# Moving waits in a fused attention and Fourier-mixing kernel: masks, last fold, square root, requests and closing work

## The chip, the core and the metric

The kernel runs on one core of a Trainium2 chip. The core has five engines that run their own instruction queues in order: TensorE (PE, matrix products into PSUM), VectorE (DVE), ScalarE (ACT), GpSimd (POOL) and SyncE (SP), which here only issues transfers. They meet through semaphores. The metric is the device time of one execution in microseconds (us); lower is better.

## The reference

```python
scores = scale * np.matmul(q, k.transpose(0, 1, 3, 2))   # q, k, v: (8, 8, 576, 64)
thresh = np.max(scores, axis=-1, keepdims=True) - tau
scores = np.where(scores >= thresh, scores, -1e9)
attn = softmax(scores)                                    # denominator + 1e-9
x = np.matmul(attn, v)                                    # heads laid side by side: (8, 576, 512)
u = x + np.real(np.fft.fft(np.fft.fft(x, axis=1), axis=2))
un = (u - mean(u)) / np.sqrt(var(u) + 1e-6)               # over the last axis
out = u + np.maximum(un @ w_ch1, 0.0) @ w_ch2             # w_ch1: 512 x 2048, w_ch2: 2048 x 512
```

Everything is float32.

## The kernel before

The eight batches go through two pipelines that are interleaved by hand on each engine's queue.

**Attention.** A batch has four pairs of heads, a pair five steps (t = 0 to 4): four tiles of 128 query rows for both heads, and one for the last 64 rows of both. Step i has its scores in PSUM (L427, L433; tile `sc`), then in `softmax_first` the row maxima on VectorE (L506) and the exponentials and the threshold on ScalarE (L512, L516), in `softmax_second` the masks, which also sum the rows, on VectorE (L527) with the reciprocal (L534), and in `softmax_third` the scaling on ScalarE (L540). `weights_in_parts` transposes the weights of the step before on TensorE (L578, L596; tiles `pe`, `pw`) and copies them out on ScalarE (L584, L598). `values_in_parts` multiplies them with v at t = 3 and at t = 1 of the next pair (L627, tile `pv`) and copies the result to x on ScalarE (L634). `prep_pair` (t = 3) transposes k and q of the next pair on VectorE (L398 to L401) and then calls `load_pair` for the pair behind it, which has 8 transfers on SyncE's queue (L134); `load_v` has four (L149, L152).

**Mixing.** When a pair is complete, `fold_rows` adds and subtracts its rows in mirrored places (L678, L683); for the last pair of a batch this is on VectorE and `mixing` follows at once: more folds (L709 to L740), products with the Fourier tables (L750, tile `py`; L767, L771, tile `pa`), sums and differences (L787, L788) and the addition to x that gives u (`add`, L790, L794), on GpSimd.

**Channels.** Of the 4608 rows of u, groups of 512 go through the two products. The first group is done plainly; its weights are then kept in memory in the form for a fast multiplication scheme (seven products for eight, for the second product in two levels). Groups 1 to 8 run `two_level`: sums of u on GpSimd (`u_form`, L1085), seven products for each of four parts (L1161, tile `ph`, evictions at L1098, L1170, L1103), and 49 products of the second level (L1278, tile `po`), whose left sides are formed at L1142 and L1119 on VectorE and GpSimd and whose results are gathered in `v_..` (evictions L1290, L1292, L1295; sums L1209, L1268) and added to u with the factor 1/sqrt(var) (`rows.add`, L861). `Rows.load` transposes u into rows (L834, L839, L840, statistics L842); `Rows.factors` has the square root on ScalarE, [...] loads of tables stand before and behind it (L850, L853), and the reciprocal (L854). Weight blocks of 1 MB are read again for every group into three buffers (`ensure`, L1034), each requested when the buffer's last product has been issued.

The loop for steps 40 and later sets the order: scores, values, softmax_first, then `fill`, which takes the next piece of `mixing` and as many pieces of `two_level` as a budget of work allows, masks, half of the transposes, `fill`, the other half, scaling, `fill`. Folds advance at `fold_more`, which is also called as background work inside `two_level`. All single-bank products share four PSUM banks (tag `mm`); the scores have two buffers of two banks. Behind the loop `fill` alone runs the rest; the sums and additions of the last group are all done behind its last product:

```python
        for v in (v_22, v_21, v_12):
            pending.extend(gather(V if last else P, v))
        ...
        if g == NG - 1:
            while pending:
                tick()
```

Of the kernel before, what the change touches and what calls it, by code (L numbers as in the profile page):

```python
# [47 lines left out]
def kernel(  # L48
# [12 lines left out]
    nc = tc.nc  # L61
# [329 lines left out]
    def prep_pair(n):  # L391

        q_raw, k_raw = loaded.pop(n)
        kT = sb.tile([128, D + S], FP32, tag="kT", name="kT")
        nc.vector.transpose(kT[:, D : D + S], k_raw[:, :])  # L398
        nc.vector.transpose(kT[64:128, 0:D], k_raw[64:128, 512:S])
        qT = sb.tile([128, S], FP32, tag="qT", bufs=1, name="qT")  # L400
        nc.vector.transpose(qT[:, :], q_raw[:, :])  # L401
        heads[n] = (qT, kT, v_in[n % 2])
        if n + 1 < B * NPAIR:
            load_pair(n + 1)

    def prep_ends(n):
# [312 lines left out]
    def mixing(b):  # L719
# [58 lines left out]
        for t in range(2):  # L778
            cols = slice(128 * t, 128 * t + 128)
            tmp = sb.tile([128, 3, KH], FP32, tag="tmp", bufs=1, name="tmp")  # L780
            low, high, sin = (tmp[:, c, :] for c in range(3))
            pb = over_seq(y_o, 1, cols, 128)
            nc.scalar.copy(sin, pb[:, 0:KH])
            yield MIX / 11
            pa = over_seq(y_e, 0, cols, 128)

            nc.vector.tensor_tensor(out=low, in0=pa[:, 0:KH], in1=sin, op=ALU.subtract)  # L787
            nc.vector.tensor_tensor(out=high, in0=pa[:, 0:KH], in1=sin, op=ALU.add)  # L788
            def add(c, rows, first, second, eng=nc.gpsimd):
# [270 lines left out]
    def two_level(g, rows):  # L1060
# [21 lines left out]

        def u_form(out_, in0, in1):
            for c in range(2):
                nc.gpsimd.tensor_tensor(  # L1085
                    out=out_[:, c], in0=in0[:, c], in1=in1[:, c], op=ALU.subtract
                )

# [119 lines left out]
        def plus(eng, to, other):  # L1208
            return lambda: eng.tensor_tensor(out=to, in0=to, in1=other, op=ALU.add)  # L1209
# [15 lines left out]
            ]  # L1225

        def finish(i, n, v):
            v = v.rearrange("p (j n) -> p j n", n=128)
            cols = slice(256 * n, 256 * n + 256)
            second = v[:, 3]  # L1230
            second = bass.AP(
                tensor=second.tensor, offset=second.offset,
                ap=[list(second.ap[0]), [-128, 2], [1, 128]],
            )
            return [
                lambda: rows.add(2 * i, cols, v[:, 1:7:5]),
                lambda: rows.add(2 * i + 1, cols, second),
            ]
# [27 lines left out]
        at_slots(4, (0, 2), finish(0, 0, v_11))  # L1266
        at_slots(
            5, (0,), [lambda: P.tensor_tensor(out=v_12, in0=v_u, in1=v_22, op=ALU.add)]  # L1268
        )
        at_slots(6, (0, 1), [plus(P, v_22, v_u), plus(P, v_21, v_u)])  # L1270
        for at, m in enumerate(L1):
            for jn, j in enumerate(J):
                if jn in (0, 4):
                    bank = ps.tile([128, 512], FP32, tag="mm", bufs=4, name="po")
                to = bank[:, 128 * (jn % 4) : 128 * (jn % 4 + 1)]
                right_ = block(g, True, 7 * at + jn)
                for s in range(4):
                    nc.tensor.matmul(  # L1278
                        to, lefts[m][j][:, s], right_[:, 128 * s : 128 * (s + 1)],
                        start=jn in (0, 4) and s == 0, stop=s == 3, skip_group_check=True,  # L1280
                    )
                if jn in (3, 6):
                    size = 512 if jn == 3 else NV - 512
                    src = bank[:, 0:size]

                    def here(v):
                        return v[:, 0:512] if jn == 3 else v[:, 512:NV]

                    if m in (1, 5, 4):
                        nc.scalar.copy(here({1: v_u, 5: v_22, 4: v_21}[m]), src)  # L1290
                    elif m == 2:
                        V.tensor_tensor(out=here(v_11), in0=here(v_u), in1=src, op=ALU.add)  # L1292
                    else:
                        to = here(v_12 if m == 3 else v_u)
                        V.tensor_tensor(out=to, in0=to, in1=src, op=ALU.add)  # L1295
# [12 lines left out]
        last = g == NG - 1  # L1308
        for v in (v_22, v_21, v_12):
            pending.extend(gather(V if last else P, v))  # L1310
# [5 lines left out]
        if g == NG - 1:  # L1316
            while pending:
                tick()
        yield 2048

    pending = []

    def tick():

        for _ in range(2):
            if pending:
                pending.pop(0)()
# [14 lines left out]
            fold_more()  # L1342

    late = []


    mixes = []
# [17 lines left out]
    total = B * per_batch  # L1365
    groups = 0
# [220 lines left out]
    for i in range(2 * per_batch, total + 3):  # L1587


        n, t = divmod(i, NT)  # L1590
        values = iter(())
        if i < total:
            scores(i)
        if t == 3 and i < total:
            values = values_in_parts(n, 0)
        elif t == 1 and n > 0:
            while folds:
                fold_more()
# [18 lines left out]
        if t > 2 or i % per_batch == 1:  # L1617
            fold_more()
        fill()
        if i % per_batch == 1:  # L1620
            fold_more()
        next(weights, None)
        if i < total:
            softmax_third(i)
            if t == 1:
                prep_ends(n)
            if t == 2 and n + 1 < B * NPAIR:
                scale_q(n + 1)
            if t == 3 and n + 1 < B * NPAIR:
                prep_pair(n + 1)  # L1630
        if i % per_batch == 1:
            fold_more()
        fill()
    per_slot = cost(0) / 40
    while mixes or work:
        fill()
# [46 lines left out]
```

## Time and profile before

| what | value |
|---|---|
| time, median of 3 runs | 1615.85 us (1615.81 to 1615.89) |
| span of the profiled execution | 1612.0 us |
| TensorE busy | 1541.6 us |
| VectorE, ScalarE, GpSimd busy | 1086.8, 906.5, 826.6 us |
| TensorE's mean granted clock | 0.987 of full |
| read from memory, written | 207.5 MB, 29.6 MB |
| last matmul ends | 1600.7 us |

A line of a timeline gives the start, the length of a run of like instructions, the engine, the line of the code, output and inputs, how many there were and, in brackets, how long the engine had been idle and what released it. A line of the waits gives who waited for whom: us in total, times, longest. A line of the windows view gives a stretch, the busy time in it, the clock that TensorE was granted (1.00 is full), the share of the transfer engines in use and GB/s. A busy TensorE is not one at its peak: at half clock its matmuls take longer and count as busy.

### The profile page before, as it was taken

To read this page: it belongs to the slowest core of one execution; us is meant where nothing else is said; L and a number is where in the kernel's file an instruction comes from. 1 tells how busy PE (TensorE), PEld (TensorE's weight loads), DVE (VectorE), ACT (ScalarE), POOL (GpSimd) and SP (SyncE) were. 2 spreads that over 40 slices of the span, in tenths; PEclk is the share of its full clock that TensorE was granted. 3 is DMA by queue.
4 is the path that set the end of the run, shared out by engine and by line. 5 is a ranking of instruction groups with operands and counts; after the bars stand their busy time and mean duration, and the time that the engine had idled before them with its cause. 6 is when DMAs were issued, how large, how long until landed. Compare 5 with 4: busy or idle time off the path is not lost.

```text
span 1612.0 us, 27099 instructions
## 1 busy us (share of the span) xinstructions
PE 1541.6 (96%) x9770; PEld 1191.6 (74%) x9770; DVE 1086.8 (67%) x2141; ACT 906.5 (56%) x1873; POOL 826.6 (51%) x1035
## 2 busy tenths in 40 slices
PE   8998989999999999999999999999999999899997
PEld 4555445556778778877787878787887778789997
DVE  7997886846868566766577566856676656526446
ACT  5774665554654667656666666666665665133121
POOL 6784664034354542646254724464264526547746
PEclk9999999999999999999999999999999999999999
DMA  6423221654945354634454445535463435446655
GB/s 158 129 57 114 75 75 36 185 169 146 293 140 178 108 161 124 200 108 133 140 173 140 124 128 153 183 113 158 127 183 104 146 113 184 164 156 234 235 195 187
DMA packets 245499, 239.05 MB, mean 148 GB/s; under 512 B 196947, under 2 KB 214869, under 8 KB 225014
## 3 DMA queue, kind: packets, MB, share of 16 engines
q1 hardware_dynamic: 242854, 237.02, 47.7%
q8 instruction: 78, 1.28, 0.3%
q10 hardware_dynamic: 2512, 0.30, 0.2%
q14 instruction: 55, 0.45, 0.1%
HBM read 207.50 MB, written 29.62 MB: 147 GB/s over the span
## 4 chain that ended last, share of the span: by engine, by line
PE 75%; DVE 15%; ACT 5%; POOL 2%; issue 2%; DMA 2%; SPq 0%; DVEq 0%; ACTq 0%; POOLq 0%
PE ph L1161 23%; PE po L1278 18%; PE pv L627 8%; PE sc L427 7%; PE pw L596 6%; PE po L899 3%; PE ph L875 2%; DVE e L467 2%; PE sc L433 1%; PE py L750 1%; DVE neg L506 1%; ACT e L512 1%; PE pa L767 1%; DVE e L527 1%; DVE neg L451 1%
## 5 line engine op out<-in xcount | busy, mean ns | idle before, releaser
L512 ACT ACTIVATE e<-sc,neg 128x576 f32<-128x576 f32 x216 | 158.4, 733 | 137.0 <-DVE neg L506 137.0
L1278 PE MATMUL po<-w,w_all 128*128 128x128 f32 x1792 | 230.1, 279 | 3.6 <-DMA w<-f 3.6
L506 DVE TENSOR_REDUCE neg<-sc 128x1 f32<-128x576 f32 x216 | 154.1, 750 | 110.5 <-PE sc L427 104.8
L1278 PEld LDWEIGHTS po<-w,w_all 128*128 128x128 f32 x1792 | 215.0, 194 | 12.5 <-issue 6.9
L1098 DVE TENSOR_TENSOR hs<-ph,hs 128x512 f32<-128x512 f32 (+1 forms) x128 | 105.2, 822 | 173.1 <-PE ph L1161 118.3
L1107 POOL TENSOR_TENSOR w<-hs 128x512 f32<-128x512 f32 x32 | 41.7, 1307 | 323.3 <-ACT hs L1103 247.6
L427 PE MATMUL sc<-kT,qT 64*128 64x288 f32 x1024 | 176.2, 437 | 14.6 <-DVE e L467 8.3
L596 PE MATMUL pw<-ident,e 128*128 128x128 f32 x1152 | 170.0, 274 | 13.9 <-ACT x_first L634 5.8
L1161 PE MATMUL ph<-u_t,w 128*128 128x256 f32 x768 | 180.5, 382 | 0.6 <-DMA w<-f 0.5
L598 ACT COPY e_t<-pw 128x512 f32<-128x512 f32 x256 | 147.7, 592 | 51.9 <-PE pw L596 50.7
L527 DVE SCALAR_TENSOR_TENSOR e<-sc,thr,e 128x576 f32<-128x576 f32 x216 | 168.1, 811 | 12.4 <-ACT thr L516 12.4
L540 ACT ACTIVATE e<-e,den 128x576 f32<-128x576 f32 x216 | 157.7, 776 | 30.5 <-DVE den L534 30.4
L596 PEld LDWEIGHTS pw<-ident,e 128*128 128x128 f32 x1152 | 134.7, 141 | 33.1 <-ACT x_first L634 7.5
L1161 PEld LDWEIGHTS ph<-u_t,w 128*128 128x128 f32 x768 | 141.5, 190 | 23.2 <-issue 4.8
L1161 PE MATMUL ph<-w_all,w 128*128 128x256 f32 x672 | 156.4, 382 | 0.0
L427 PEld LDWEIGHTS sc<-kT,qT 64*128 64x128 f32 x1024 | 96.4, 189 | 73.3 <-issue 32.0
L1161 PEld LDWEIGHTS ph<-w_all,w 128*128 128x128 f32 x672 | 124.1, 190 | 21.4 <-issue 6.4
L1103 ACT ACTIVATE hs<-hs 128x512 f32<-128x512 f32 (+1 forms) x96 | 74.0, 771 | 114.1 <-DVE hs L1098 112.9
L1209 POOL TENSOR_TENSOR w_all<-w_all 128x128 f32<-128x128 f32 (+2 forms) x161 | 117.4, 746 | 23.4 <-DVE w_all L1295 10.2
L1278 PE MATMUL po<-w,hs 128*128 128x128 f32 x960 | 127.0, 279 | 0.0
L1278 PEld LDWEIGHTS po<-w,hs 128*128 128x128 f32 x960 | 117.0, 194 | 5.1 <-issue 3.3
L790 POOL TENSOR_TENSOR u_t<-x,tmp 128x289 f32<-128x289 f32 (+1 forms) x47 | 34.9, 743 | 97.4 <-DVE tmp L787 97.4
(217 smaller groups left out, 2982.9 us busy)
## 6 DMA issues: line engine op xcount, KB each, us to landing
w<-f SPq DMA_DIRECT2D x152, 1024.0 KB, 4.9
hs<-in_moe_w_ch_dram SPq DMA_DIRECT2D x23, 512.0 KB, 4.4
q_in<-in_q_dram SPq DMA_DIRECT2D x128, 72.0 KB, 2.5
out_dram<-u SPq DMA_DIRECT2D x36, 256.0 KB, 2.3
k_in<-in_k_dram SPq DMA_DIRECT2D x124, 72.0 KB, 2.5
v_in<-in_v_dram SPq DMA_DIRECT2D x64, 128.0 KB, 2.6
f<-w SPq DMA_DIRECT2D x14, 512.0 KB, 3.6
f<-w SPq DMA_DIRECT2D x7, 1024.0 KB, 4.2
```

The costliest lines, as they stand in the source:

```text
L427: nc.tensor.matmul(sc[j][:, c, 0:HALF], qT[hp, 128 * t : 128 * t + 128], kT[hp, k0 + HALF * c : k0 + HALF * (c + 1)], start=True, stop=True,)
L506: nc.vector.tensor_reduce(out=neg[:, j : j + 1], in_=sc[j][:, :, 0:HALF], axis=AXIS_XY, op=ALU.max, negate=True,)
L512: nc.scalar.activation(out=ej, in_=sc[j][:, :, 0:HALF], func=ACT.Exp, bias=neg[:, j : j + 1], scale=1.0)
L527: nc.vector.scalar_tensor_tensor(out=ej, in0=sc[j][:, :, 0:HALF], scalar=thr[:, j : j + 1], in1=ej, op0=ALU.is_ge, op1=ALU.mult, accum_out ...
L540: nc.scalar.activation(out=e[:, S * j : S * (j + 1)], in_=e[:, S * j : S * (j + 1)], func=ACT.Copy, scale=den[:, j : j + 1],)
L596: nc.tensor.transpose(pw[:, c, :], e[:, c0 : c0 + 128], ident[:, :])
L598: nc.scalar.copy(e_t[:, 4 * j : 4 * j + 4, qs], pw[:, :, :])
L627: nc.tensor.matmul(pv[64 * j : 64 * j + 64, 0:m], vt[:, 2 * c + j, :], e_t[:, 4 * j + c, 0:m] if c < 4 else ends[:, 0, 0:m], start=(c == 0 ...
L1098: nc.vector.tensor_tensor(out=to, in0=bank, in1=to if other is None else other, op=ALU.add)
L1161: nc.tensor.matmul(bank[:, 256 * q : 256 * q + 256].rearrange("p (two n) -> p two n", two=2), left[:, 256 * c + 128 * q : 256 * c + 128 * ...
L1209: return lambda: eng.tensor_tensor(out=to, in0=to, in1=other, op=ALU.add)
L1278: nc.tensor.matmul(to, lefts[m][j][:, s], right_[:, 128 * s : 128 * (s + 1)], start=jn in (0, 4) and s == 0, stop=s == 3, skip_group_check ...
```

## The change

Seven edits, all of order or place; no product is added or removed.

- The masks of a step (`softmax_second`) come directly behind its exponentials, ahead of the evictions of the first `fill`.
- The fold of the last pair of a batch no longer stands in the common list but has places of its own in steps t = 1 and 2 of the next batch.
- The square root moves from right behind the last row tile to behind the step's scaling, or to the first addition that needs it.
- q and k are requested at the end of the t = 4 step instead of behind the transposes at t = 3, v at the end of t = 2 instead of in t = 1.
- Behind the loop a `fill` does channel work first and a piece of mixing second.
- In the last batch the addition for x3 is on VectorE, and so is `u_form` of the last two groups.
- The last group's sums and additions are done while its last seven products run; of those, the last three are evicted one by one, so that behind the last one there are an eviction, an addition of 128 columns and one store.

```diff
@@ prep_pair
-        if n + 1 < B * NPAIR:
+        if n + 1 < B * NPAIR and not late:
             load_pair(n + 1)
@@ mixing
-            def add(c, rows, first, second, eng=nc.gpsimd):
+            def add(c, rows, first, second, eng=None):
+                if eng is None:
+                    eng = nc.vector if b == B - 1 and c % 2 else nc.gpsimd
@@ two_level
         def u_form(out_, in0, in1):
-                nc.gpsimd.tensor_tensor(
+                (nc.vector if g >= NG - 2 else nc.gpsimd).tensor_tensor(
...
         def finish(i, n, v):
+            if wanted:
+                wanted.pop().factors()
...
-        at_slots(6, (0, 1), [plus(P, v_22, v_u), plus(P, v_21, v_u)])
+        if g < NG - 1:
+            at_slots(6, (0, 1), [plus(P, v_22, v_u), plus(P, v_21, v_u)])
+        else:
+            at_slots(6, (0, 0), [plus(V, v_22, v_u), plus(P, v_21, v_u)])
+            at_slots(6, (1, 1, 1, 1, 1), gather(V, v_22))
+            at_slots(6, (2, 2), finish(1, 1, v_22))
+            at_slots(6, (2, 2, 3, 3, 3), gather(V, v_21))
+            at_slots(6, (4, 4), finish(1, 0, v_21))
+            at_slots(6, (4,), [stores(2, 3)])
...
                     if at == 3:
-                        rows.factors()
+                        wanted.append(rows)
...
-        last = g == NG - 1
+        if g == NG - 1:
+            w = v_12.rearrange("p (j n) -> p j n", n=128)
+            rows.add(0, slice(384, 512), w[:, 6])
+            rows.store(0)
+            return
@@ fill
-        if mixes:
+        if mixes and not ended:
             mix(1)
...
+        if mixes and ended:
+            mix(1)
@@ the loop from step 40 on
         if i < total:
             softmax_first(i)
+            softmax_second(i)
         next(values, None)
         if i % per_batch == 2:
-            while folds:
-                fold_more()
+            for _ in last_fold:
+                pass
             start_batch(i // per_batch - 1)
-        if t == 1 and n + 1 < B * NPAIR:
-            load_v(n + 1)
         fill()
         if t == 1:
-            folds.append(fold_rows(n - 1))
-        if i < total:
-            softmax_second(i)
+            if n % NPAIR:
+                folds.append(fold_rows(n - 1))
+            else:
+                last_fold = fold_rows(n - 1)
+                next(last_fold)
...
+        if wanted:
+            wanted.pop().factors()
         if i % per_batch == 1:
-            fold_more()
+            next(last_fold)
         fill()
+        if t == 2 and n + 1 < B * NPAIR:
+            load_v(n + 1)
+        if t == 4 and n + 2 < B * NPAIR:
+            load_pair(n + 2)
+    ended.append(True)
```

More of the change, by code (lines that the diff above doesn't have):

```diff
@@ L1265, in two_level @@
         at_slots(2, (0, 1, 2, 3, 4), gather(P, v_11))
-        at_slots(4, (0, 2), finish(0, 0, v_11))
+        at_slots(4, (2, 4), [lambda n=n: finish(0, 0, v_11)[n]() for n in range(2)])
         at_slots(
@@ L1269, in two_level @@
         )
-        at_slots(6, (0, 1), [plus(P, v_22, v_u), plus(P, v_21, v_u)])
+        if g < NG - 1:
[8 more added lines that the diff above has]
+            w = v_12.rearrange("p (j n) -> p j n", n=128)
+            at_slots(6, (4,) * 4, [
+                plus(V, w[:, 1:5:3], twice(w[:, 0])), plus(V, w[:, 6], w[:, 2]),
+                plus(V, w[:, 6], w[:, 4]), lambda: rows.add(0, slice(256, 384), w[:, 1]),
+            ])
+            second = bass.AP(
+                tensor=w.tensor, offset=w[:, 3].offset, ap=[list(w.ap[0]), [-128, 2], [1, 128]]
+            )
+            at_slots(6, (5,) * 4, [
+                plus(V, w[:, 5], w[:, 4]), plus(V, w[:, 2:4], twice(w[:, 5])),
+                lambda: rows.add(1, slice(256, 512), second), stores(1),
+            ])
         for at, m in enumerate(L1):
             for jn, j in enumerate(J):
-                if jn in (0, 4):
+                cut = g == NG - 1 and m == 3
+                if jn in (0, 4) or cut and jn > 4:
                     bank = ps.tile([128, 512], FP32, tag="mm", bufs=4, name="po")
-                to = bank[:, 128 * (jn % 4) : 128 * (jn % 4 + 1)]
+                c0 = 0 if cut and jn > 4 else 128 * (jn % 4)
+                to = bank[:, c0 : c0 + 128]
                 right_ = block(g, True, 7 * at + jn)
@@ L1279, in two_level @@
                         to, lefts[m][j][:, s], right_[:, 128 * s : 128 * (s + 1)],
-                        start=jn in (0, 4) and s == 0, stop=s == 3, skip_group_check=True,
-                    )
-                if jn in (3, 6):
-                    size = 512 if jn == 3 else NV - 512
-                    src = bank[:, 0:size]
+                        start=(jn in (0, 4) or cut and jn > 4) and s == 0, stop=s == 3,
+                        skip_group_check=True,
+                    )
+                if jn in (3, 6) or cut and jn > 3:
+                    first, end = (0, 512) if jn == 3 else (512, NV)
+                    if cut and jn > 3:
+                        first, end = 128 * jn, 128 * jn + 128
+                    src = bank[:, 0 : end - first]
                     def here(v):
-                        return v[:, 0:512] if jn == 3 else v[:, 512:NV]
+                        return v[:, first:end]
                     if m in (1, 5, 4):
@@ L1307, in two_level @@
                 yield 2048
-        last = g == NG - 1
+        if g == NG - 1:
+            w = v_12.rearrange("p (j n) -> p j n", n=128)
+            rows.add(0, slice(384, 512), w[:, 6])
+            rows.store(0)
+            return
         for v in (v_22, v_21, v_12):
-            pending.extend(gather(V if last else P, v))
+            pending.extend(gather(P, v))
         pending.extend(finish(1, 1, v_22))
@@ L1315, in two_level @@
         pending.append(stores(0, 1))
-        if g == NG - 1:
-            while pending:
-                tick()
         yield 2048
     pending = []
+    wanted = []
     def tick():
@@ L1344 @@
     late = []
+    ended = []
     mixes = []
@@ L1602 @@
             softmax_first(i)
+            softmax_second(i)
         next(values, None)
         if i % per_batch == 2:
[L1605 to L1606 removed]
+            for _ in last_fold:
+                pass
             start_batch(i // per_batch - 1)
[L1608 to L1609 removed]
         fill()
         if t == 1:
[L1612 to L1614 removed]
+            if n % NPAIR:
[3 more added lines that the diff above has]
+                next(last_fold)
         weights = weights_in_parts(i - 1) if i <= total else iter(())
         next(weights, None)
[L1617 removed]
+        if t > 2:
             fold_more()
@@ L1630 @@
                 prep_pair(n + 1)
+        if wanted:
+            wanted.pop().factors()
         if i % per_batch == 1:
-            fold_more()
+            next(last_fold)
         fill()
+        if t == 2 and n + 1 < B * NPAIR:
[3 more added lines that the diff above has]
+    ended.append(True)
     per_slot = cost(0) / 40
```

## The prediction

> **What bounds the kernel now.** I began with the page: engines' busy time and the chain that ended last.
>
> ```profile
> PE 1541.6 (96%) x9770; PEld 1191.6 (74%) x9770; DVE 1086.8 (67%) x2141; ACT 906.5 (56%) x1873; POOL 826.6 (51%) x1035
> ...
> PE 75%; DVE 15%; ACT 5%; POOL 2%; issue 2%; DMA 2%; SPq 0%; DVEq 0%; ACTq 0%; POOLq 0%
> ```
>
> TensorE sets the end. Of 1612.0 us it is not busy for 70.4, of which 11.3 lie behind its last matmul. The change removes no matmul, so it can win only idle time, what idle time does to the clock, and the end. Then the waits by engine, PE's own (us, times, longest), those that the late part of the program has:
>
> ```profile
> PE sc L427 <- DVE e L527: 6.4, 6, 2.7
> PE pw L596 <- ACT x_first L634: 5.8, 5, 1.4
> PE py L750 <- DVE f L731: 5.1, 2, 4.6
> PE ph L1161 <- POOL t_room L1085: 4.1, 1, 4.1
> PE po L1278 <- DMA w<-f: 3.6, 1, 3.6
> ```
>
> PE's timeline places them. The loop that the change rearranges begins near 332 us. From there I count 28.5 us of gaps: 1.5 at 410 to 417; 3.6 at 480; 11.3 around the five batch boundaries (517 to 524, 688, 865 to 872, 1038 to 1045, 1211 to 1218) and 2.4 in small ones near them (757, 840, 856, 1028, 1201); 5.05 at 1382; 4.1 at 1410; 0.5 at 1506. The windows view of 2 us (PE busy, clock, DMA share, GB/s) shows what a long gap costs besides itself:
>
> ```profile
> 481.00:483.00 2.00, 0.00 (x0) 0.68 0.99 410
> 483.00:485.00 2.00, 1.67 (x8) 0.50 1.03 434
> 485.00:487.00 2.00, 2.00 (x10) 0.50 1.00 422
> 487.00:489.00 2.00, 2.00 (x10) 0.61 0.18 74
> 489.00:491.00 2.00, 2.00 (x18) 1.00 0.00 0
> ```
>
> Matmuls resume at 483.3 but the clock stays at half until about 488.5: 5.2 us at half, 2.6 lost. The same windows elsewhere give a loss of about 1.7 behind the 2.7 us gap at 688, 2.9 behind 1382, 1.5 behind 1410. So 8.7 us more. Gaps up to 1.7 us show no dip, one of 2.06 us (at 18) does.
>
> Why the load was late, from SyncE's timeline (start, length, what):
>
> ```profile
> 445.83 15.96 SPq L1034 DMA_DIRECT2D w<-f  x3
> 473.97 1.96 SPq L134 DMA_DIRECT2D q_in<-in_q_dram  x4
> 475.97 2.12 SPq L134 DMA_DIRECT2D k_in<-in_k_dram  x4
> 478.19 1.85 SPq L1034 DMA_DIRECT2D w<-f  x3
> ```
>
> The q request waits 12.1 us for the transposes that free its buffer, eight requests take 4.1 us, and only then comes the weight block that PE wants at 479.7.
>
> At a boundary (DVE, ACT, PE at 1216):
>
> ```profile
> 1216.21 1.41 DVE L506 TENSOR_REDUCE neg<-sc 128x1 f32<-128x576 f32 x2
> ...
> 1218.50 0.37 ACT L634 COPY x_first<-pv 128x256 f32<-128x256 f32 x1
> ...
> 1218.92 0.66 PE L596 MATMUL pw<-ident,e 128*128 128x128 f32 x4 [1.42 <-ACT x_first L634]
> ```
>
> VectorE runs without a pause from 1205.67 to 1217.62; its late maxima delay the exponentials, these the copy that frees PE's bank. And the end:
>
> ```profile
> 1600.74 0.56 DVE L1295 TENSOR_TENSOR w_all<-w_all,po 128x384 f32<-128x384 f32 x1 [1.99 <-PE po L1278]
> 1601.21 4.66 DVE L1209 TENSOR_TENSOR w_all<-w_all 128x256 f32<-128x256 f32 x15
> 1605.79 2.46 DVE L861 SCALAR_TENSOR_TENSOR u<-w_all,rstd,u 128x256 f32<-128x256 f32 x6
> 1607.13 1.80 SPq L868 DMA_DIRECT2D out_dram<-u  x4
> ```
>
> [...] L1142 takes 0.68 us alone and up to 2.44 beside GpSimd. [...] the trace has 1.28 twice for each square root. [...]
>
> **The change part by part.**
>
> Later requests. q and k are now asked for at the end of the t=4 step (buffer long free), v at the end of t=2. In the built program the weight loads stand ahead of them. They still arrive two to three steps (8.6 us each) before use, against 4.1 us of issue and 2.5 to landing. The stall at 480 goes: 3.6 + 2.6 = 6.2. Elsewhere a weight load may now stand behind 4 us of requests, but it is asked for two blocks (8 products of 0.9 us, with attention work between some 14) ahead and lands in 4.9: hidden.
>
> Masks behind the exponentials. In the queue of VectorE they pass the evictions of the first fill. New wait: first exponential to the threshold, about 0.4 us a step; behind it stand those evictions, which PE's four banks wait for. Where values are multiplied first (t=1, t=3), VectorE is idle then anyway (2.9 us at 1127.7), so this costs nothing. In t=4 steps of the ph stage I work out a delay of 1.4 us for L1098 (1137.67 to 1139.1), through ACT's relu to the copy of ends (1138.94 to 1140.5), and PE wants that bank at 1140.2: 0.3 to 0.4 us, once or twice a batch, 6 batches: 2.5 us lost (0 to 6). Won: score banks come free 2 to 4 us sooner, so the sc waits at 410, 517, 688 and their like go. At 410 to 417 I count 1.2 of 1.5.
>
> Boundary: masks, last fold, square root. Before, VectorE idled 3.2 us for ACT's copy of u and 0.7 for the root between 1194.9 and 1199.8. After, the masks (1.5) and half (1.8) fill that, but the reciprocal now waits behind ACT's two e_t copies, two scalings (1.44), load (1.28) and root (0.30): I get 1203.55, VectorE idle from about 1201.4, 2.1 us. Sum of idling 3.3 instead of 3.9, and work of the same size; less overlap with GpSimd may give 0.9. So the maxima at 1216.21 come 0.3 to 1.5 sooner, and PE, which loses the 0.57 and 0.63 gaps before, waits 1.1 to 2.3 at the bank instead of 1.42. The gap mostly moves. I take 0.7 a boundary: 3.5 in all, including the dip at 688.
>
> Short-end order. Behind the loop a fill now does its work before the mixing: three products (0.89 each) go ahead of the first py. VectorE's fold at L731, ready at 1387.15, stays, as the same L1142 pair (beside GpSimd) stands ahead. The gap of 5.05 becomes 2.4; dip 1.7 instead of 2.9: 3.9 won (3 to 8).
>
> Adds and u_form on VectorE. GpSimd's serial run from 1403.84 to 1413.9 (twelve adds of 0.7 to 0.8, then t1) splits. Adds for x3 run on VectorE by about 1405.5, freeing tmp 1.3 sooner; x1 is then done by about 1408.2 on GpSimd and t1 on VectorE by 1408.5 to 1409, before PE wants it at 1409.9. The row adds end about 1410.9, t2 1411.9, against PE at 1411.6. The gap and its dip go: 4.1 + 1.5 = 5.6. The first ph evictions wait for eight u_forms (0.35 each, to 1413.4), and PE wants m=7's bank at 1415.2: hidden.
>
> End. All sums and all additions to u but the last stand ahead of the last eviction now; VectorE has 1.6 + 2.0 us idle there, but gets one 896-wide sum (1.0) from GpSimd and two more evictions. Working its list from 1596.44: end of the last addition 1606.1 without, 1607.2 with a slowing by GpSimd, instead of 1608.25. Only one store is then left, not four of 1 MB together. 1.9 won (1 to 3).
>
> Small gaps (757, 840, 1028): 0.6 won. Sum: 6.2 + 1.2 + 3.5 + 3.9 + 5.6 + 1.9 + 0.6 - 2.5 = 20.4, less 1 for waits not foreseen: 19. 1615.85 - 19 = 1597.
>
> **Rivals.**
> 1. Gaps move and merge. At each boundary one gap of 2.3 us brings a dip of 1.7: 4.0 instead of 2.6, lost 1.4 at four of them; bank waits at their 6. Then 6.2 + 5.6 + 1.9 + 1.2 + 3.9 - 5 - 6 = 8: 1608. For it: the unbroken VectorE run at 1206. Against: no other work was added.
> 2. VectorE gets ahead everywhere: of 28.5 + 8.7 + 2 about 33 go, only the py gap stays: 1583. For it: VectorE is 67% busy and the masks fill idle time.
> 3. Slower: the masks' wait stops the evictions in most steps. 0.2 us of PE in each of 120 steps is 24, more than the 20 won: 1620. For it: four banks, all busy. Against: at 1120.98 a mask already waits 0.8 us for the threshold, with no PE gap.
>
> **How the numbers follow.** Forecast 0.62, rival 1 0.18, rival 2 0.13, rival 3 0.07. The range takes in rivals 1 and 2 about half: 1583 to 1609. Faster by over 0.2% (below 1612.6) 0.88; same 0.05; slower 0.07.
>
> **What would show it.** PE idle near 45 us instead of 70; no wait of po for w at 480; no clock at 0.50 after 1410; sc waits for L527 gone, but bank waits (x_first) left at 1.1 to 2.3; a py gap near 2.4; 9 to 10 us behind the last matmul. Wrong if a wait for ACT's root or for new evictions appears on PE's list, or a dip at every boundary.

## The result, and the profile after

| | before | after |
|---|---|---|
| time, median | 1615.85 us | 1631.27 us (1630.36 to 1632.28, 3 runs) |
| ratio | 1 | 1.0096, 95% interval 1.0073 to 1.0119 |
| span of the profiled execution | 1612.0 us | 1628.5 us |

The change makes the kernel 15.4 us slower. The forecast was 1597, and the time lies above the range (1583 to 1609). The page of the changed kernel, engines and chain:

```profile
PE 1549.9 (95%) x9770; PEld 1194.2 (73%) x9770; DVE 1101.7 (68%) x2165; ACT 907.7 (56%) x1873; POOL 813.2 (50%) x1014
...
PE 67%; DVE 18%; ACT 9%; issue 3%; POOL 2%; DMA 1%; SPq 0%; DVEq 0%; ACTq 0%; POOLq 0%
```

The same 9770 products are busy 8.3 us longer, and TensorE idles 78.6 us instead of 70.4. Both count. The longer busy time is clock: half of the time in which TensorE is busy at half clock is 24.7 us here and was 15.6, 9.1 more. That this half is lost is an estimate: eight `po` products take 1.06 us at full clock (1213.75 in this trace) and 1.91 in a stretch at 0.50 (1239.33). TensorE's waits, of the late part of the program (us, times, longest):

```profile
PE pw L596 <- ACT x_first L634: 11.3, 6, 2.3
PE py L750 <- DVE f L731: 11.1, 11, 2.6
PE ph L1163 <- DVE hs L1100: 5.3, 5, 2.0
PE pw L596 <- DVE hs L1100: 2.4, 2, 2.1
PE ph L1163 <- ACT ends L584: 2.0, 11, 0.4
```

The waits of `sc` for the masks (L527) are off the list, and the waits of `po` for `w` at 480 and of `ph` for `t_room` too. In their place stand the fold, the bank and the evictions at L1100 (L1098 before, where they had one wait of 0.3). The ledger of both traces, gaps over 0.25 us from the timeline and lost clock (half of the time in which TensorE is busy in the stretches at 0.50; what it idles there is a gap already), in us; the boundaries, where a batch's mixing begins, are called b2 to b6:

| place | before: gaps, clock | after: gaps, clock |
|---|---|---|
| 400 to 430 | 1.55, 0 | 3.12, 1.71 |
| about 480 | 3.64, 2.61 | 0.96, 0 |
| five batch boundaries | 12.98, 1.71 | 19.70, 12.80 |
| other places up to 1380 | 0.71, 0 | 3.02, 0 |
| behind the loop | 9.63, 4.45 | 5.90, 1.71 |
| gaps under 0.25 us from 315 on | 2.6, 0 | 5.4, 0 |

Before: 39.9; after: 54.3; 14.4 of the 16.5 us between the spans. In the first 315 us, where TensorE's products have the same order, it is 1.0 more, behind the last product 0.4 less; some 1.5 stay unplaced. At the boundaries 17.8 us are lost more, and 11.1 of them are clock. At one of them, b6, TensorE's timeline reads:

```profile
1214.64 0.60 PE L836 MATMUL pn<-ident,u_t 128*128 128x128 f32 x4
...
1231.20 0.44 PE L750 MATMUL py<-dim_c,f 128*128 128x65 f32 x2
1232.25 0.43 PE L750 MATMUL py<-dim_c,f 128*128 128x64 f32 x2 [0.62 <-DVE f L731]
1233.69 0.49 PE L750 MATMUL py<-dim_c,f 128*128 128x128 f32 x2 [1.01 <-DVE f L731]
...
1237.57 1.12 PE L596 MATMUL pw<-ident,e 128*128 128x128 f32 x4 [2.19 <-ACT x_first L634]
```

From the transposes `pn` to the `pw` behind the bank wait it takes 22.93 us; before, 22.37 (1196.55 to 1218.92). So the boundary itself is only 0.56 us longer. TensorE gets to its first `py` 16.56 us behind `pn`, 2.45 sooner than before (1215.56 - 1196.55 = 19.01), and then waits. VectorE keeps its pace: the maxima of step t = 3, on which the rest hangs, start 20.22 us behind `pn` (1234.86), before 19.66 (1216.21). What is new is that three gaps lie within 6 us.

That VectorE comes no sooner has one more reason in the trace. Two of the folds now lie beside additions of GpSimd:

```profile
1229.03 1.38 POOL L1144 TENSOR_TENSOR w_all<-hs,w_all 128x512 f32<-128x512 f32 x1 [3.48 <-PE sc L427]
1229.20 1.54 DVE L735 TENSOR_TENSOR f<-sums 128x304 f32<-128x304 f32 x1
1230.38 1.49 POOL L1121 TENSOR_TENSOR hs<-hs,w 128x512 f32<-128x512 f32 x1
1230.67 1.53 DVE L731 SCALAR_TENSOR_TENSOR f<-sums,factors 128x304 f32<-128x304 f32 x1
```

Before they took 0.45 and 0.53 us (1213.05 and 1213.42), and GpSimd's last addition ahead of them had ended at 1212.91. With the masks early, in the run with the root back (b6) and in the one with the masks alone (b5), each takes 1.54; with the masks late, in the run without the three moves (b5) and in the fastest (b6), they take 0.46 or 0.45, and 0.53. Against these 2.1 us, L710 takes 0.79 instead of 1.75. No run separates this overlap from the order of the queue, so how much of the waits for L731 is its work stays open.

The clock comes on top. The windows view, in pieces of 3.41 us, the length of the shortest stretch at 0.50 in this trace (us, PE busy, clock, DMA share, GB/s):

```profile
1229.83:1233.24 3.41, 2.24 (x18) 1.00 0.04 7
1233.24:1236.66 3.42, 1.68 (x11) 1.00 0.21 38
1236.66:1240.07 3.41, 2.50 (x12) 0.50 0.66 269
1240.07:1243.49 3.42, 3.42 (x18) 0.50 0.28 80
1243.49:1246.90 3.41, 3.41 (x25) 1.00 0.94 148
```

Behind a piece with 1.74 us of idle time the clock is at half for two whole pieces, in which TensorE is busy for 5.92 us: 2.96 lost. The same boundary of the kernel before never has so much idle time in one piece:

```profile
1208.77:1212.19 3.42, 2.79 (x22) 1.00 0.65 268
...
1215.60:1219.01 3.41, 1.99 (x18) 1.00 0.27 41
```

Its largest idle time is 1.42, and the clock stays at 1.00.

### The profile page after: what moved, and what is told of

It reads as the page before. It is cut to its first block, busy times and chain, and to the rows that moved or that the text cites. A ratio compares the mean times of both kernels' runs of the same rounds, so it can differ in the third digit from the quotient of the medians.

```text
span 1628.5 us, 27053 instructions
## 1 busy us (share of the span) xinstructions
PE 1549.9 (95%) x9770; PEld 1194.2 (73%) x9770; DVE 1101.7 (68%) x2165; ACT 907.7 (56%) x1873; POOL 813.2 (50%) x1014
## 4 chain that ended last, share of the span: by engine, by line
PE 67%; DVE 18%; ACT 9%; issue 3%; POOL 2%; DMA 1%; SPq 0%; DVEq 0%; ACTq 0%; POOLq 0%
PE ph L1163 19%; PE po L1304 16%; PE pv L627 8%; PE sc L427 7%; PE pw L596 5%; PE po L901 3%; ACT e L512 2%; PE ph L877 2%; DVE e L527 2%; DVE e L467 2%; DVE hs L1100 2%; PE py L750 1%; DVE neg L506 1%; PE pa L767 1%; ACT hs L1105 1%
## 5 line engine op out<-in xcount | busy, mean ns | idle before, releaser
L527 DVE SCALAR_TENSOR_TENSOR e<-sc,thr,e 128x576 f32<-128x576 f32 x216 | 169.1, 816 | 69.6 <-ACT thr L516 69.6
L1100 DVE TENSOR_TENSOR hs<-ph,hs 128x512 f32<-128x512 f32 (+1 forms) x128 | 105.0, 821 | 140.0 <-PE ph L1163 90.8
L596 PE MATMUL pw<-ident,e 128*128 128x128 f32 x1152 | 175.5, 280 | 21.8 <-ACT x_first L634 11.3
L427 PE MATMUL sc<-kT,qT 64*128 64x288 f32 x1024 | 169.8, 434 | 9.6 <-DVE e L467 8.3
L1304 PE MATMUL po<-w,hs 128*128 128x128 f32 x960 | 130.5, 284 | 0.0
L1304 PEld LDWEIGHTS po<-w,hs 128*128 128x128 f32 x960 | 120.6, 199 | 5.1 <-issue 4.1
```

The lines of the kernel that those rows point to most:

```text
L427: nc.tensor.matmul(sc[j][:, c, 0:HALF], qT[hp, 128 * t : 128 * t + 128], kT[hp, k0 + HALF * c : k0 + HALF * (c + 1)], start=True, stop=True,)
L527: nc.vector.scalar_tensor_tensor(out=ej, in0=sc[j][:, :, 0:HALF], scalar=thr[:, j : j + 1], in1=ej, op0=ALU.is_ge, op1=ALU.mult, accum_out ...
L596: nc.tensor.transpose(pw[:, c, :], e[:, c0 : c0 + 128], ident[:, :])
L1100: nc.vector.tensor_tensor(out=to, in0=bank, in1=to if other is None else other, op=ALU.add)
L1304: nc.tensor.matmul(to, lefts[m][j][:, s], right_[:, 128 * s : 128 * (s + 1)], start=(jn in (0, 4) or cut and jn > 4) and s == 0, stop=s == ...
```

## The experiments

My theory after the comparison was that the later root makes VectorE wait, that this delays the fold, and that the fold's gaps and the bank's gap together bring the half clock. The rivals: the masks ahead of the fold, the fold's own place, or too much work on VectorE whatever the order.

### One part added, or one taken back

**Later requests alone, on the kernel before.**

```diff
-        if n + 1 < B * NPAIR:
+        if n + 1 < B * NPAIR and not late:
             load_pair(n + 1)
...
-        if t == 1 and n + 1 < B * NPAIR:
-            load_v(n + 1)
...
+        if t == 2 and n + 1 < B * NPAIR:
+            load_v(n + 1)
+        if t == 4 and n + 2 < B * NPAIR:
+            load_pair(n + 2)
```

> The kernel before with one part of the change alone: q and k asked for at the end of the t=4 step, v at the end of t=2. If step 1 of the prediction is right, the stall of po at 480 (3.64 us of gap and two windows of half clock, 3.4 us) shrinks to the 0.7 us that the changed kernel shows there, and nothing else moves: 1615.85 - 6.3 = 1609.5 us. If later requests only put the weight blocks behind other transfers, the win is under 2 us: 1614 or more.

1608.08 us, ratio 0.9952 (0.9938 to 0.9965): 7.8 us won. The gap and the half clock at 480 are gone from its trace: from the same products in both traces, the stretch from 470 to 500 is 6.3 us shorter. Against what I expected, something else moves too: from 400 to 440 it is 2.4 us shorter, as the waits of 0.78 (`sc` for L527, 410.36) and 0.77 (`pw` for L634, 417.44) are gone. The boundaries are those of before (0.57, 0.63 and 1.42).

**The root back, on the changed kernel.**

```diff
                     if at == 3:
-                        wanted.append(rows)
+                        rows.factors()
```

> The changed kernel with the square root of the row factors back where it was, right at the request for the rows. Theory root: VectorE's wait of 2.31 us for the root (idle ahead of L856 at 1221.63) makes the fold at L731 late, and this makes the two py gaps (0.62 and 1.01) and, with the bank gap of 2.19 behind them, two windows of half clock (3.4 us lost) at each of five boundaries. Then the py gaps go and at most one half window stays: 3.3 to 5 us a boundary, 1631.3 - 17 to 22 = 1609 to 1614. Theory masks: the masks ahead of the fold make it late; the root's place is worth under 1 us a boundary: 1627 to 1631. Theory load: VectorE has too much work at the boundary once TensorE runs ahead, whatever the order: 1627 to 1631 too.

1631.45 us, ratio 1.0093 (1.0078 to 1.0109), the same as the changed kernel's 1.0096. My theory fell. VectorE's timeline of this run shows why:

```profile
1220.06 0.18 DVE L856 RECIPROCAL rstd<-rstd 128x4 f32<-128x4 f32 x1 [0.39 <-ACT rstd L852]
...
1221.01 3.14 DVE L683 TENSOR_TENSOR f<-half 128x143 f32<-128x143 f32 x4
```

The wait for the root falls from 2.31 to 0.39 us, but the four folds at L683 take 3.14 us instead of the 1.04 of the changed kernel (0.55 at 1218.76 and 0.49 at 1221.72), now that they run at the time of two GpSimd additions:

```profile
1221.26 2.72 POOL L1121 TENSOR_TENSOR hs<-hs,w 128x512 f32<-128x512 f32 x2
```

In the changed kernel the same two additions run from 1219.01 to 1221.66, and two of the folds start ahead of them, two behind them. L1142 in the kernel before shows the like: 0.68 us at 1209.49, where GpSimd is idle, and 2.44 at 1383.25 beside GpSimd's L1268 and L1142. Here 2.1 us are given back for the 1.9 won.

**The masks back, and the fold back, each on the changed kernel.** The masks move to where they were, behind the first `fill` and the new fold; the last fold goes back to the common list.

```diff
             softmax_first(i)
-            softmax_second(i)
...
                 next(last_fold)
+        if i < total:
+            softmax_second(i)
```

> The changed kernel with the masks back behind the first fill. Theory root: the boundaries stay as they are and only the new waits of ph and pw (1.01, 2.11 with a half window of 1.71, 0.25, 0.39, 1.95, against 1.55 us of old sc and pw waits) go: about 6 us, 1625. Theory masks: the boundary loss of about 20 us goes as well: 1606 to 1612. Theory load: nothing but the 6 us: 1625.

> The changed kernel with the last fold of a batch back in the common list of folds, its parts where they were. Theory root, masks and load: the fold still waits in VectorE's queue behind the root, under 2 us: 1629 to 1632. A fourth theory, that the fold's own place makes it late: the py gaps and half windows at five boundaries go, 17 to 22 us: 1609 to 1614.

Masks back: 1612.21, ratio 0.9978 (0.9968 to 0.9987), 19 us less than changed. Fold back: 1627.6, ratio 1.0077 (1.0061 to 1.0093), 3 us less and within reach of the changed kernel's interval. So the masks decide. With masks back and root and fold moved, the boundary is still no good one: gaps of 1.74 (`po` for `w_all`), 1.74 (`pw` for `ends`) and, at two of the last three, about 1.0 (`pw` for x_first), where before had 0.57, 0.63 and 1.42. The mean granted clock of this profile is 0.987, that of the changed kernel 0.981.

### The masks by themselves

**All three moves taken back; then the masks alone.** The first kernel keeps the later requests and the edits at the program's end; the second adds only the masks directly behind the exponentials.

```diff
-                        wanted.append(rows)
+                        rows.factors()
...
-                last_fold = fold_rows(n - 1)
-                next(last_fold)
...
+            folds.append(fold_rows(n - 1))
```

> The changed kernel with all three moves inside the attention steps taken back (masks, last fold, root): what stays is the later requests and the work at the end of the program. From the ledger of gaps and half windows: the later requests won 7.9 of 1615.9 when alone, and the end shows 4.2 less at the py gap behind the loop, 3.0 less around 1410 and 0.4 less behind the last matmul: 1600.4 us. The prediction's own steps for the end (3.9 + 5.6 + 1.9 = 11.4) give 1596.6. If the masks were of use anywhere, this kernel must show their old waits and be above 1603.

> The changed kernel with root and last fold back, the masks still directly behind the exponentials; against the kernel without all three it shows the masks alone. Theory masks (they alone let TensorE run ahead of VectorE at a boundary, so that the waits fall together in front of py and pw and bring half windows, and they alone delay the ph evictions): as slow as the changed kernel, 1625 to 1632. Theory pair (the masks hurt only together with the later root or the fold's own place): near the kernel without all three plus the 6 us of ph waits, 1604 to 1610.

Without the three: 1604.62, ratio 0.9931 (0.9918 to 0.9944). With the masks: 1631.8, ratio 1.0107 (1.0092 to 1.0121). The move of one call costs 27 us; root and last fold, added to it, cost nothing more. In the two profiles, `pn` to the maxima of t = 3 is 19.98 us without and 20.08 with the masks (1021.04 to 1041.02 and 1036.20 to 1056.28): VectorE's pace at a boundary is the same in sum, and with the masks TensorE gets to its first `py` 17.13 us behind `pn` instead of 18.94: it runs ahead into the boundary.

The first kernel came out 4 us above the 1600.4 that I had expected. Its boundary gaps are 0.57, 0.96 and 1.82 instead of 0.57, 0.63 and 1.42, and the mean granted clock of its profile is 0.988, where the later requests alone have 0.99. The likely cause is a small edit in the change of which I had made nothing, for later requests alone leave these gaps as they were and the other edits lie behind the loop: the first product's additions (`finish(0, 0, ..)`) go from slots 0 and 2 to 2 and 4, in every group. An addition of 0.48 us (L863) now stands ahead of the last L731 there. The run that puts them back is told below, on another kernel.

**Which masks.** From the kernel with the masks alone, those of the three steps around a boundary go back (in the other run those of the t = 4 steps, with `t != 4` as the condition):

```diff
             softmax_first(i)
-            softmax_second(i)
+            if i % per_batch not in (1, 2, 3):
+                softmax_second(i)
```

> The kernel with the masks alone (1631.8), with the masks of the three steps around a boundary (steps 1 to 3 of each batch) back behind the first fill, all others still directly behind the exponentials. Theory boundary: the boundary part of the loss (gaps and half windows) is made by the masks of these steps; left are the ph waits of about 8 us: 1604.6 + 8 = 1612.6 (1610 to 1616). Theory everywhere: masks in all steps push VectorE's work together, and the boundary suffers from that: 1624 or more.

> The kernel with the masks alone (1631.8), with the masks of the t=4 steps back behind the first fill. Theory t=4: there the mask waits 1.27 us for the threshold and holds the eviction L1100 back by 1.6 us; TensorE loses 0.72 us in two such steps of a batch (six batches: 8.6 us), in some of them 1 to 2.1 us, and half windows behind these: with 7.6 us found at the boundaries 19 to 20 are left for it: 1611 to 1614. Theory everywhere: all steps lose a little, the t=4 steps only their fourth or fifth: 1624 or more.

Boundary steps back: 1624.18, ratio 1.0043 (1.0027 to 1.0058), 7.6 us of the 27; I had expected 19, so most of the harm is elsewhere. The t = 4 steps back: 1616.36, ratio 1.0006 (1.0000 to 1.0013), 15.4 us; I had expected 19 to 20. In a t = 4 step of the changed kernel:

```profile
1154.78 0.27 PE L578 MATMUL pe<-ident,e 128*128 128x128 f32 x1
...
1155.50 0.82 DVE L527 SCALAR_TENSOR_TENSOR e<-sc,thr,e 128x576 f32<-128x576 f32 x1 [1.27 <-ACT thr L516]
...
1156.62 0.67 DVE L1100 TENSOR_TENSOR hs<-ph,hs 128x512 f32<-128x512 f32 x1
1157.33 0.63 ACT L1105 ACTIVATE hs<-hs 128x512 f32<-128x512 f32 x1 [1.87 <-DVE hs L1100]
1157.35 0.66 PE L596 MATMUL pw<-ident,e 128*128 128x128 f32 x4
1157.87 0.25 ACT L584 COPY ends<-pe 128x128 f32<-128x128 f32 x1
...
1158.17 0.70 PE L1163 MATMUL ph<-u_t,w 128*128 128x256 f32 x2 [0.16 <-ACT ends L584]
```

The mask waits 1.27 us for the threshold, as ScalarE is at a relu before. The eviction L1100, whose bank is ready, stands behind it. Against the transpose `pe` (1154.78; 1137.47 before) it starts 1.84 us later, before 0.20 (1137.67). TensorE waits twice for it: at `pw` for the bank that L1100 frees, which starts 2.57 instead of 2.28 us behind `pe`, and at `ph` for the one that the copy of `ends` frees, 3.39 instead of 2.72. In the kernel before the eviction was ahead of the mask:

```profile
1137.67 0.69 DVE L1098 TENSOR_TENSOR hs<-ph,hs 128x512 f32<-128x512 f32 x1 [0.74 <-PE ph L1161]
...
1138.28 0.81 DVE L527 SCALAR_TENSOR_TENSOR e<-sc,thr,e 128x576 f32<-128x576 f32 x1
...
1139.75 0.60 PE L596 MATMUL pw<-ident,e 128*128 128x128 f32 x4
...
1140.19 0.38 PE L1161 MATMUL ph<-u_t,w 128*128 128x256 f32 x1
```

Product by product, the trace of the run with the boundary masks back falls behind that of the run without the three moves by 0.79 us at such a step, at two of them in most batches. In the late waits of the run with the t = 4 masks back, `pw` for L1100 (2.4 us in the changed kernel) is gone, and `ph` for `ends` has 0.9 instead of 2.0. Against the run with the masks alone it gains 7.6 us at these steps and 3.4 from 425 to 440, where the gap of 2.11 and the half clock behind it (3.41 us in the changed kernel) go; that is 11.0 of the 12.3 us between these two profiles (the medians differ by 15.4). The gaps of 1.01 at 408 and 1.95 at 766 stay (1.00 and 1.95), so they come from other steps.

### Is it the clock?

**Useless work in the gap, on the changed kernel.** In the step behind a boundary, in the free quarter of the bank that `pe` has:

```diff
         nc.tensor.transpose(pe[:, 0, :], e[:, 512:640], ident[:, :])
+        if late and i % per_batch == 2:
+            for _ in range(16):
+                nc.tensor.transpose(pe[:, 3, :], ident[:, :], ident[:, :])
```

> The changed kernel with 16 transposes of the unit matrix, whose result nobody reads, on TensorE directly ahead of the pw that waits for x_first behind each boundary (1.8 us of useless work in a gap of 2.19). Theory clock: the wait itself is not shortened, but TensorE is no longer idle in it, so the half windows (3.41 us lost at b4, b5, b6 and the one before, 1.7 at the first) become fewer or vanish: 1631.3 - 8 to 15 = 1616 to 1623. Theory waits: the time is lost by the waits alone, and the half clock behind them is made up in later idle time: 1630 to 1636, as the useless work can only delay.

1622.61, ratio 1.0048 (1.0036 to 1.0060): 8.7 us less for 96 transposes more (six places, one of them ahead of b2). The trace at the boundary shown above (this kernel's lines are 3 higher):

```profile
1228.97 0.30 PE L578 MATMUL pe<-ident,e 128*128 128x128 f32 x1
1229.11 1.91 PE L581 MATMUL pe<-ident 128*128 128x128 f32 x16
1231.46 0.66 PE L599 MATMUL pw<-ident,e 128*128 128x128 f32 x4 [0.44 <-ACT x_first L637]
```

`pw` starts 2.49 us behind `pe`, exactly as in the changed kernel (1235.08 to 1237.57). The wait is as long as it was; only the clock differs: 0.989 in the mean of the profile instead of 0.981. Half clock is gone at two of the five boundaries and shorter at the other three: 5.1 us lost there instead of 12.8. From the same products in both traces, the five boundaries are 9.2 us shorter together. Elsewhere, where nothing was filled, half clock moved as well: it came up behind the 1.95 at 761 (1.7 us longer) and is missing at 431 and 1410 (1.6 and 1.2 shorter).

**The bank wait taken away, on both.** In the changed kernel ScalarE has nothing to do for 7.05 us at this place; it waits with the exponentials of t = 3 in hand while the copies that free TensorE's banks stand behind them. So in that step the first `fill` goes ahead of the maxima and exponentials:

```diff
-        if i < total:
+        boundary = i % per_batch == 3
+        if i < total and not boundary:
             softmax_first(i)
...
         fill()
+        if i < total and boundary:
+            softmax_first(i)
```

> The kernel without the three moves, and in the step behind a boundary ScalarE gets the copies that free TensorE's banks (x_first, y_e) ahead of the exponentials, which there wait for late maxima. Theory bank: the gap of pw on x_first (1.42 us at four boundaries) is only an order of ScalarE's queue, which idles ahead of these exponentials; it goes: 5 to 6 us less than without, about 1595. Theory load: VectorE's late maxima set the pace, the gap comes back one or two blocks later as a wait for scaled exponentials: under 1 us less.

> The changed kernel with the same copies ahead of the exponentials (and masks) in the step behind a boundary. Theory clock: most of the loss at a boundary is not the gaps (3.8 us against 2.6 before) but the half windows that they bring [...] (0 before, 3.4 us lost after). With the bank gap of 2.19 gone only the py gaps of 1.6 stay, and the half windows go at most boundaries: 10.9 of gaps and 9 to 14 of clock less, 1606 to 1611. Theory load: the bank gap comes back as another wait nearby: 1627 to 1631.

On the kernel without the three moves: 1598.51, ratio 0.9895 (0.9882 to 0.9908), 6 us less; the bank gap falls from 1.82 to 0.53. On the changed kernel: 1614.06, ratio 0.9990 (0.9982 to 0.9998), 17 us less; the bank gap falls from 2.19 to 0.90 or under 0.25, and from the same products in both traces the five boundaries are 3.0, 2.1, 3.2, 3.9 and 4.0 us shorter, all of the 16.2 us between the spans. The edit moves the maxima of that step on VectorE too; they start 0.6 us later and this shows no cost. Expected were 1606 to 1611: right in kind, 3 us short. At b4 to b6 nothing like the gap came back later; at b3, on the kernel without the three moves, one of 1.23 did.

### The rest, and the fastest

**The first product's additions back in slots 0 and 2**, on the kernel with the copies first; then `u_form` shared between the two engines; then early masks in the remaining steps only.

```diff
-        at_slots(4, (2, 4), [lambda n=n: finish(0, 0, v_11)[n]() for n in range(2)])
+        at_slots(4, (0, 2), finish(0, 0, v_11))
...
-                (nc.vector if g >= NG - 2 else nc.gpsimd).tensor_tensor(
+                (nc.vector if g >= NG - 2 and c else nc.gpsimd).tensor_tensor(
...
+        early = t != 4 and i % per_batch not in (1, 2, 3)
```

> The kernel without the three moves and with the copies first (1598.5), and the additions of the first product of a group back at the early slots. In the trace these additions stand on VectorE ahead of the last fold; later slots made the sc wait 0.96 instead of 0.63 and the bank wait 1.82 instead of 1.42. Theory: 0.7 us a boundary, five boundaries, and perhaps a half window less: 1594 to 1597. Rival: with the copies first the bank wait is only 0.5, so that the later slots cost nothing more: 1598.

> The kernel of the run before, with the u_form of the last two groups shared: one of two halves on VectorE, one on GpSimd. The waits of ph for w_all (0.96) and for hs (1.83) behind the last mixing come from VectorE, which has eight halves to do there. Theory: with half of them on GpSimd both waits shrink, 1 to 2.5 us less. Rival: GpSimd is busy with additions until then, as it was before the change (gap of 4.07): 2 us more.

> The fastest kernel so far (1595.4: later requests, the end of the program, copies first, additions of the first product early) with the masks directly behind the exponentials in the steps that are neither t=4 nor at a boundary. If all the harm sits in those two, this is 1594 to 1597, no different, for no score bank is waited for outside the boundaries. If the early masks cost in every step, it is 1600 or more.

Additions back: 1595.42, ratio 0.9877 (0.9864 to 0.9889), 3.1 us less, though the two intervals touch. In the two traces four of the five boundaries gain 0.3 to 0.4 us; of the 4.6 us between the spans, most is half clock ahead of 315 us and behind the loop (mean granted clock 0.992 instead of 0.989). It is the fastest kernel here: 20 us under before, 36 under changed. At b4 to b6 its only gaps over 0.25 us are 0.57 and 0.63, and there is no half clock in the loop but 1.71 us at 684. In its list of waits `py` for L731 is left once, with 2.6 us behind the loop, and `pw` for x_first is gone.

`u_form` shared: 1597.23, ratio 0.9884 (0.9871 to 0.9897), no different; the two waits of 0.96 and 1.83 turn into one of 3.36 for `t_room` on GpSimd. Early masks in the remaining steps: 1603.23, ratio 0.9920 (0.9908 to 0.9933), 8 us slower (7 by the ratios), where I had expected no difference. Gaps of 1.01, 0.39 and 1.96 at `ph` come back, all ahead of b4 (5.0 us in the profiles' stretches that hold them); from b4 on the two traces are alike. In no combination tried here did the early masks help.

## Why the prediction was wrong, step by step

**Later requests** (6.2 us): right; the stretch at 480 became 6.3 us shorter. The other part of the 7.8 measured lies from 400 to 440, where this edit alone takes away the two waits of which I had put 1.2 down to the masks; the one of 0.77 is back in three of the later runs.

**Masks behind the exponentials** ("2.5 us lost (0 to 6)", 1.2 won): the step that failed. The masks alone cost 27.2 us. In the t = 4 steps the mechanism is the one I described, at the place I described, L1098 to relu to the copy of ends; the size was too small by a factor of six. I took 0.3 to 0.4 us "once or twice a batch"; it is 0.79, in two steps of most batches, as `pw` waits for the bank of the eviction as well, and ahead of 431 a gap of 2.11 with 3.41 us at half clock behind it comes on top. Measured by taking back: 15.4 us at t = 4, 7.6 at the boundaries, and about 4 left for the other steps if the parts add up (27.2 less these two; 7 to 8 measured on the fastest kernel), with the gaps of 1.01 and 1.95 among them. That VectorE "is idle then anyway" at t = 1 and t = 3, so that the masks cost nothing there, proved right only outside the boundaries and from b4 on; idle is the engine and not its queue, for it idles in front of the threshold while a ready eviction stands behind.

**Boundaries** ("I take 0.7 a boundary", 3.5 won): wrong, the second step that failed; 17.8 us more in the ledger. I had the pieces: VectorE's fold is the bound there, the gap "mostly moves", the root's wait is 2.1 (2.31 measured), the bank wait 1.1 to 2.3 (2.19). I did not draw the conclusion. Letting the `sc` waits go brings TensorE 2.45 us sooner to a fold that comes no sooner, so three gaps that were 7 to 10 us apart fall together. This is rival 1, which I gave 0.18, with a larger dip: 2.6 to 3.0 us lost instead of 1.7 at four of the five boundaries. The waits of `py` for L731 were not foreseen at all, though in the kernel before the last of these folds ended at 1215.44, just ahead of the first `py` at 1215.56.

Behind it lies a reading that was already wrong on the trace of the kernel before: "gaps up to 1.7 us show no dip". The piece ahead of one of its half clocks has only gaps of 1.12 and 0.20 us, 1.32 of idle time in all:

```profile
102.77:106.18 3.41, 2.09 (x12) 1.00 0.01 2
106.18:109.59 3.41, 3.41 (x14) 0.51 0.03 5
```

I had measured gaps one by one; here two short ones lie in the piece ahead of the half clock.

**Short-end order** (gap of 5.05 to 2.4): right, 2.58. **Adds and `u_form` on VectorE** (5.6 won): half right; the 4.08 gap goes, but waits of 0.96 for `w_all` and 1.83 for L1100 appear, the second of which I had called hidden. **End** (1.9 won): 0.4. The last product ends at 1617.56, and 10.9 us follow (11.3 before; I had said 9 to 10), since VectorE's list from 1613.36 to 1625.2 has no pause, and its sum of 256 columns at 1614.69 takes 2.19 us beside a GpSimd sum of 2.94 us (0.42 at 1618.78, where GpSimd is idle). With the three moves taken back, requests, order, adds and end together win 0.69%, 11.1 us, and the later slots of the first product's additions, which I had not priced, hold back up to 3 more; the steps had summed to 17.6 (6.2 + 3.9 + 5.6 + 1.9).

**Rival 3**, slower at 1620 through the masks' wait in most steps, had 0.07. It was right on the side and on the culprit; the loss that it spread as "0.2 us of PE in each of 120 steps" lies mostly in the t = 4 and boundary steps, and part of it is clock (11.1 us at the boundaries and 1.7 at 431 in the ledger).

**What stays open.** Why the fold's own place gains 3 us when taken back with the masks early, while the pair of root and fold costs 8 with the masks back, was not taken apart. Nor was the part of GpSimd in the longer folds at the boundaries, nor were the three edits of the program's end run one by one.

## What to carry to other kernels

On an engine that works its queue in order, moving an operation forward is free only if its input is ready there: look at what the operation would wait for at the new place, and what ready work stands behind it, above all evictions that free banks (here a mask that waited 1.27 us, with L1100 1.84 us behind `pe` instead of 0.20). Where another engine sets the pace of a stage, removing a wait ahead of it only moves the idle time, and where it moved next to other idle time here, half clock made it dearer (by 2.96 us at b6, by the estimate above). Before reordering work, see whether an idle engine holds back a copy that frees a buffer: one change of order that paid here (6 us, and 17 on the changed kernel) let two copies go ahead of exponentials that were waiting anyway.

## What the runs showed of the hardware

In the traces of the kernel before and of the changed one, the half clock follows pieces of time and not single gaps. All stretches at 0.50, nine and thirteen, begin at whole multiples of 3.41 us from each other, and all but the last of each trace, which stands behind the last product, are 3.41 or 6.83 us long. Cut into such pieces, from 8 us to the last product, the two traces together show:

| clock in the piece | TensorE's idle time in it, us | pieces | next piece at 0.50 |
|---|---|---|---|
| 1.00 | up to 1.25 | 872 | 0 |
| 1.00 | 1.29 to 1.83 | 24 | 7 |
| 1.00 | 1.92 or more | 13 | 13 |
| 0.50 | up to 0.40 | 20 | 0 |
| 0.50 | 0.90 or more | 6 | 6 |

What decides from 1.29 to 1.83 these traces do not show: 1.29 us was followed by half clock at 693 in the kernel before, 1.42 at b6 was not. The gap of 1.95 at 764 in the changed kernel lies across two pieces, with 1.77 us in the first, and no half clock follows. The two traces also differ where no edit has reached: up to 297 us TensorE, VectorE, ScalarE and GpSimd have the same work in the same order in both, yet half clock loses 6.8 us there before and 8.5 after by the same estimate, and the product that starts at 296.1 us in the kernel before starts at 297.1 in the changed one.
